# A long convolution and a gated MLP, forward and backward on one core: the filter's first transform over whole rows instead of halves, another opening, and one load moved behind another

## The chip, the cores and the metric

The kernel runs on one core of one Trainium2 chip. The metric is the device time of one execution in microseconds (us). Times in the profile are microseconds from the start of the span unless they are marked ns.

## The reference

The kernel computes the output of a block and all its gradients from a given gradient of the output. S is 2048, D is 1024, F is 3584, and everything is bfloat16 at the edges:

```python
xn = layernorm(x)                                     # [S, D]
# A: short convolution of k with 4 taps, times v, then a long convolution with a filter per channel
kv  = shift(k, shift_k) * v
y   = irfft(rfft(pad(kv)) * rfft(pad(ssm_k)))[:S] + kv * ssm_D
A   = xn * y
# B: gated MLP
gate = relu(xn @ W_gate); up = xn @ W_up
B   = (gate * up) @ W_down
out = x + A + B
# returned: out, and by vjp(grad_out) the gradients of x, k, v, shift_k, ssm_k, ssm_D, W_gate, W_up, W_down
```

## The kernel before

There are two branches in one instruction stream, and TensorE is shared by both.

The MLP branch (class LnMlp) has four phases. In `hidden`, the 3584 hidden columns are worked in 7 blocks of 512 for each half of the rows, 14 blocks in all; a block computes for each of 8 row tiles the gate product ps_g, the up product ps_u and the gradient product ps_h, each as 8 matmuls of 128x128 by 128x512 (`gemm8`, L788). ScalarE takes the relu of ps_g (L885) and copies ps_h (L958), VectorE multiplies (L891, L893, L959), and the results go to DRAM as h_d and ug_d. These products share a pool of four accumulators. The later phases are `grad_down` and `grad_in` (ps_d and ps_w, L1039 and L1052), `out_phase` (ps_o, L1197) and `grad_x` (ps_x, L1266).

The first block of `hidden` also holds the layer norm. `layer_norm` is a generator that works the 16 row tiles of x in ten chunks, `LN_CHUNKS = (1, 1, 1, 1, 2, 2, 2, 2, 2, 2)`: row sums on ScalarE (L726), centring on VectorE (L749), squares on ScalarE (L726), a root on ScalarE (L757), a few one-column operations and the scaling on VectorE (L770). In the first chunk, both sums are shared by the two engines, half a row each. `flip_xn` then transposes a row tile on TensorE (L820) and VectorE copies it to xnT (L822); the first tile is copied in two halves. Ahead of all this, `warm` runs 24 products whose results nobody reads. The loads of x wait in SP's queue in the order in which the program issues them: chunks 0 and 1, the gate weights, chunks 2 and 3, the up weights, chunk 4, four transposing loads of the down weights (wdT), two of the output's gradient (goT), chunk 5.

The convolution branch (class ABranch) works the 1024 channels in 8 groups of 128. A transform of length 4096 is done as products with tables: `fwd1` (a product with a table R over 64 rows), a transposition on VectorE (`flip`, L313), `fwd2`, products of the transforms on VectorE (`cmul`), and inverses. All its matmuls are recorded at L72, its ScalarE copies at L76, its VectorE operations at L80 and its loads at L88. The tables are made by `tables` from sines on ScalarE during the second to third block of the MLP.

The filter of a group is loaded as hn, 128 channels by 2048 times. `h_tile` brings it into the time layout: with time = 32 q + 16 u + r, the 64 rows of half u hold q, and for each r and each u the columns hv[:, u, r, :] (64 of them, 32 elements apart) are transposed into the 64 PSUM rows of that half (L302), 32 transposes in all. ScalarE copies the result to hT. `fwd1` then multiplies R[64 u : 64 u + 64] with the 64 rows of half u, 512 columns at a time; the two halves write two banks. A chunk is four such products and two copies to the tile B.

The order is set as follows. The MLP's phases yield 1730 ns for each 8 large products, and whenever a budget is used up, one step of the convolution branch is put in. A step of a group is a pair: some TensorE work and some VectorE work (`slots`, `yield f1h, tk`), worth 1760 ns. `keep_in_program_order` and `pri.pin` fix instructions in the order written, and a scheduler places the others by priority. Before the first group, `steps` issues its loads in stages:

```python
        yield 13000
        self.load_xn(nx)      # xt, the layer norm's output for this group
        self.load_taps(nx)    # skb, the four taps
        self.pin = False
        yield 9000
        self.pri.strict = True
        hT = self.h_tile(nx)
```

xt is needed by `gate_grad`, the product gt x xt on VectorE, which in the first group stands beside the first chunk of the filter; the transform of gt (f1g) reads its result.

Of the kernel before, what the change touches and what calls it, by code (L numbers as in the profile page):

```python
# [11 lines left out]
BF16 = mybir.dt.bfloat16  # L12
# [36 lines left out]
class ABranch:  # L49
# [65 lines left out]
    def tables(self):  # L115
# [4 lines left out]
        self.FW = con.tile([P, NB1, 2, NB1], BF16, name="FW")  # L120
        self.IA = con.tile([P, 16, 2, 2, NB1], BF16, name="IA")
        self.R = con.tile([P, 2, 2, NB1], BF16, name="R")
        self.RB = con.tile([P, 64], BF16, name="RB")
        self.gs_all = con.tile([P, self.NG, 4], F32, name="gs_all")
        self.gD_all = con.tile([P, self.NG], BF16, name="gD_all")
# [18 lines left out]
        b32 = pbit(32, 1.0 / 32, "b32")  # L144
        b64 = pbit(64, 1.0 / 64, "b64")
        n1 = pbit(63, 1.0, "n1p")

        def first(n, name):
            it = self.ts.tile([P, 2, 2, NB1], I32, name="it" + name, tag="ts")
# [6 lines left out]
            nc.scalar.activation(out=tr[:], in_=it[:], func=ACT.Sin, scale=TWO_PI / 256, bias=negpi[:])  # L156
            return tr

        tr = first(n1, "R")
        V.tensor_copy(out=self.R[:], in_=tr[:])  # L160

# [132 lines left out]
    def h_tile(self, st):  # L294

        hT = self.ttile("hT")
        hv = st["hn"][:].rearrange("p r c -> p (r c)").rearrange("p (q u r) -> p u r q", u=2, r=16)
        pst = self.ps.tile([P, 16, P], BF16, name="pst", tag="aps")
        for r in range(16):
            for u in range(2):  # L300
                self.pri.now()
                self.pri.pin(self.nc.tensor.transpose(pst[64 * u:64 * u + 64, r, :], hv[:, u, r, :], self.identA[:]))  # L302
        self.act(hT[:, 0:16, :], pst[:])
        return hT

    def flip(self, st, key, src):
# [4 lines left out]
        for c0 in range(0, 64, 32):  # L311
            self.pri.late()
            self.pri.pin(self.nc.vector.transpose(out=df[:, c0:c0 + 32, :], in_=sf[:, c0:c0 + 32, :]))  # L313
            yield

    def add_D(self, st):
        for rows in (slice(0, 32), slice(64, 96)):
            b0 = st["Bh"][rows, :, 0, 0, :]
            self.tt(b0, b0, st["sD"][rows].rearrange("p (cp i) -> p cp i", i=2), ALU.add)

    def fwd1(self, st, key, src):
# [136 lines left out]
    def steps(self):  # L458

        sk_t = self.shift_rows()
        self.pin = True
        nx = self.loads_1(0)
        self.loads_2(nx)
        yield 10000
        self.load(self.sk_d, sk_t[:])
        yield 13000
        self.load_xn(nx)
        self.load_taps(nx)  # L470
        self.pin = False
        yield 9000
        self.pri.strict = True
        hT = self.h_tile(nx)
        yield 2000
        for gi in range(self.NG):
            st, nx = nx, None
            for p, d in self.slots(st, hT, gi):
                self.run(p)
                self.run(d)  # L480
                yield self.SLOT
            nx, hT = st.get("nx"), st.get("hT_next")
        self.small_outputs()

    def slots(self, st, hT, gi):
# [36 lines left out]

        ksh = st["ksh"] = self.lng.tile([P, 16, P], BF16, name="ksh")
        tk = self.taps(st, ksh, kp, [(3, 0), (2, 1), (1, 2), (0, 3)])
        f1h = self.fwd1(st, "Bh", hT)
        f1g = self.fwd1(st, "Bg", gt)
        yield f1h, (lambda: self.gate_grad(st)) if gi == 0 else None
        yield None, tk
        yield f1h, tk
        yield None, tk  # L530
        yield None, self.both(lambda: self.add_D(st), tk)
        flH = self.flip(st, "fH", st["Bh"][:].rearrange("p cp u r i -> p cp (u r) i"))
        yield f1g, flH
        yield None, flH
        yield f1g, tk
# [106 lines left out]
class LnMlp:  # L642
# [66 lines left out]
    def layer_norm(self, xn_d, jpool, jtag, spool):  # L709

        nc, D, V = self.nc, self.D, self.nc.vector

        st0 = 0
        for i, n in enumerate(self.LN_CHUNKS):
            xt = self.ln_x[i]
            self.pri.now()
            sm = spool.tile([P, 12, 4], F32, name="ln_s")
            smb = spool.tile([P, 4, 4], BF16, name="ln_b")
            f = lambda i: sm[:, i, 0:n]
            b = lambda i: smb[:, i, 0:n]  # L720
            cut = D // 2 if i == 0 else D

            def row_sums(j, k, func):

                jk = jpool.tile([P, D], BF16, name="ln_j", tag=jtag)
                self.ln_act = nc.scalar.activation(out=jk[:, 0:cut], in_=xt[:, j, 0:cut], func=func,  # L726
                                                   accum_out=sm[:, k, j:j + 1])
                if cut < D:
                    if func is ACT.Square:
                        V.tensor_tensor_reduce(out=jk[:, cut:D], in0=xt[:, j, cut:D], in1=xt[:, j, cut:D], scale=1.0,  # L730
                                               scalar=0.0, op0=ALU.mult, op1=ALU.add, accum_out=sm[:, k + 6, 0:1])
                    else:
                        V.tensor_reduce(out=sm[:, k + 6, 0:1], in_=xt[:, j, cut:D], axis=AX.X, op=ALU.add)
                return self.ln_act

            def average(k, out):
                if cut < D:
                    return V.tensor_scalar(out=out, in0=f(k), scalar1=sm[:, k + 6, 0:1], scalar2=1.0 / D, op0=ALU.add,
                                           op1=ALU.mult)
                return V.tensor_scalar(out=out, in0=f(k), scalar1=1.0 / D, scalar2=None, op0=ALU.mult)  # L740

            for j in range(n):
                total = row_sums(j, 0, ACT.Copy)
                if i != 3 and i >= 1 and j == 0:
                    self.tc.keep_in_program_order(total)
            average(0, b(0))
            V.tensor_copy(out=f(1), in_=b(0))
            for j in range(n):
                V.tensor_scalar(out=xt[:, j, :], in0=xt[:, j, :], scalar1=sm[:, 1, j:j + 1], scalar2=None,  # L749
                                op0=ALU.subtract)  # L750
                row_sums(j, 2, ACT.Square)
            yield
            var = average(2, b(1))
            if i == 2:
                self.tc.keep_in_program_order(var)
            V.tensor_scalar(out=b(2), in0=b(1), scalar1=LN_EPS, scalar2=None, op0=ALU.add)
            self.ln_act = nc.scalar.activation(out=f(4), in_=b(2), func=ACT.Sqrt)  # L757
            yield
            root = V.reciprocal(out=f(6), in_=f(4))
            if i == 1:  # L760
                self.tc.keep_in_program_order(root)
            V.scalar_tensor_tensor(out=f(5), in0=b(2), scalar=0.5, in1=f(6), op0=ALU.mult, op1=ALU.mult)
            V.scalar_tensor_tensor(out=b(3), in0=f(4), scalar=0.5, in1=f(5), op0=ALU.mult, op1=ALU.add)
            self.ln_dve = V.reciprocal(out=self.rstd[:, st0:st0 + n], in_=b(3))
            self.pri.now()
            for j in range(n):
                st = st0 + j
                for c in (0, 512) if st == 0 else (0,):
                    xc = xt[:, j, c:c + (512 if st == 0 else D)]
                    V.tensor_scalar(out=xc, in0=xc, scalar1=self.rstd[:, st:st + 1], scalar2=None, op0=ALU.mult)  # L770
                nc.gpsimd.dma_start(out=xn_d[st * P:(st + 1) * P, :], in_=xt[:, j, :])
                self.xn.append(xt[:, j, :])
            st0 += n
            yield
# [39 lines left out]
    def flip_xn(self, st):  # L814
        xT = self.act_tile("xnT", st)
        h = self.DT // 2 if st == 0 else self.DT
        for k0 in range(0, self.DT, h):
            pst = self.ps.tile([P, self.DT, P], BF16, name="pst_x", tag="bps")
            for kt in range(k0, k0 + h):
                self.pri.pin(self.nc.tensor.transpose(pst[:, kt, :], self.xn[st][:, kt * P:(kt + 1) * P],  # L820
                                                      self.ident[:]), always=True)
            copied = self.nc.vector.tensor_copy(out=xT[:, k0 * P:(k0 + h) * P],  # L822
                                                in_=pst[:, k0:k0 + h, :].rearrange("p a b -> p (a b)"))
            if st < 4:
                self.tc.keep_in_program_order(copied)
        return xT
# [9 lines left out]
    def hidden(self, first, goT, load, ln, tables, Wg, Wu, Wd, g, xn_d, h_d, ug_d):  # L836
# [6 lines left out]
        for n in range(N):  # L843
# [61 lines left out]
            def first_gate_up(sp):  # L905
# [3 lines left out]
                    chunk(1)  # L909
                gate(sp)  # L910
                yield from step()
                if sp == 0:
                    next(ln)
                    next(ln)
                    next(ln)

                def mid():
                    flip(sp + 2)
                    while len(self.xn) < 4:
                        next(ln)  # L920
                    if sp == 2:
                        chunk(2)
                up(sp, mid)
                yield from step()
                gate(sp + 1)
# [53 lines left out]
                        next(ln)  # L979

            if ahead:
                self.warm(24)
                for _ in range(3):
                    next(ln)
                next(ln)
                flip(1)
                yield from first_gate_up(0)
                yield from first_gate_up(2)
                chunk()
# [419 lines left out]
```

## Time and profile before

| | |
|---|---|
| median of 4 runs | 1922.97 us (1921.47 to 1923.59) |
| the profiled execution | 1922.91 us, span 1921.1 us |
| TensorE busy | 1912.4 us, 15710 matmuls |
| VectorE, ScalarE busy | 908.6 us, 634.0 us |
| granted TensorE clock | 1.0 from 4.8 us on |
| filter transposes, L302 | 256, 278 ns each in the mean |
| filter products ps<-hT,R | 64 of 64x512, 381 ns each in the mean |
| warm-up products, L834 | 24, 460 ns each in the mean |
| hT copies on ScalarE | 8, 1.87 us each |
| VectorE waits of TensorE for xnT (L822) | 2.0 us |

A matmul's duration is the time through the array; what it takes from TensorE's stream is the distance to the start of the next one. Two half-array matmuls can be under way side by side. The chain of waits is followed back from the last instruction.

### The profile page before, as it was taken

What the parts mean: (1) busy time and instruction counts of PE and PEld (TensorE: products, weight loads), DVE (VectorE), ACT (ScalarE), POOL (GpSimd) and SP (SyncE); (2) the same over time, 40 slices, a digit from 0 to 9 for tenths busy, and PEclk for the clock granted to TensorE, in tenths of its full rate; (3) what the DMA queues carried; (4) which work ended last, traced back from release to release, by engine and by line L of the source; (5) the groups of instructions that cost most, each with busy time, mean ns of one, the idle gap of its engine ahead of it and who ended that gap; (6) DMA issues with size and microseconds to landing.
All of it is one profiled execution on the core that took longest, in us unless ns stands there. A gap on an engine that the chain in (4) does not pass through costs nothing.

```text
span 1921.1 us, 36564 instructions
## 1 busy us (share of the span) xinstructions
PE 1912.4 (100%) x15710; PEld 886.6 (46%) x15710; DVE 908.6 (47%) x1354; ACT 634.0 (33%) x865; POOL 15.0 (1%) x37
## 2 busy tenths in 40 slices
PE   9999999999999999999999999999999999999999
PEld 4444444444444444444444444444444544444444
DVE  6777777767767754534444354310122232222222
ACT  5764354364364354354344344321000000000000
POOL 1000000000000000000000000000000000000000
PEclk9999999999999999999999999999999999999999
DMA  9975778974775872645653633376999975554553
GB/s 249 285 176 143 179 184 183 229 177 131 187 184 136 250 219 78 175 128 179 162 163 92 170 99 122 100 196 219 233 261 247 225 173 121 121 121 120 121 121 72
DMA packets 628003, 323.18 MB, mean 168 GB/s; under 512 B 458360, under 2 KB 597376, under 8 KB 627840
## 3 DMA queue, kind: packets, MB, share of 16 engines
q1 hardware_dynamic: 617344, 299.99, 62.6%
q10 hardware_dynamic: 9216, 16.65, 2.9%
q0 software_dynamic: 1280, 4.20, 0.6%
q8 instruction: 123, 2.02, 0.4%
q14 instruction: 40, 0.33, 0.1%
HBM read 143.79 MB, written 95.44 MB: 125 GB/s over the span
## 4 chain that ended last, share of the span: by engine, by line
PE 96%; DVE 1%; DMA 1%; ACT 1%; issue 0%; SPq 0%; ACTq 0%; DVEq 0%
PE ps_x L1266 20%; PE ps_w L1039 20%; PE ps_o L1197 10%; PE ps_g L788 9%; PE ps_h L788 9%; PE ps_u L788 9%; PE ps_d L1039 9%; PE ps L72 6%; PE ps_d L1052 1%; PE pst L302 1%; PE ps_w L1052 1%; ACT ln_j L726 1%; DMA ln_x<-in_A_q_dram 0%; PE ps_r L1227 0%; DMA wg<-in_B_W_gate_dram 0%
## 5 line engine op out<-in xcount | busy, mean ns | idle before, releaser
L1039 PE MATMUL ps_w<-ugs,xn_nat 128*128 128x512 bf16 x1728 | 383.3, 379 | 0.0
L788 PEld LDWEIGHTS <-xnT 128*128 128x128 bf16 x1792 | 169.6, 98 | 211.6 <-issue 11.0
L1039 PEld LDWEIGHTS <-xn_nat 128*128 128x128 bf16 x1728 | 164.7, 98 | 200.2 <-issue 7.2
L788 PE MATMUL ps_g<-wg,xnT 128*128 128x512 bf16 x896 | 206.6, 379 | 2.6 <-DVE xnT L822 2.0
L1284 ACT ACTIVATE w<-xn,m 128x512 f32<-128x512 bf16 x32 | 24.3, 806 | 553.0 <-issue 317.2
L788 PE MATMUL ps_u<-wu,xnT 128*128 128x512 bf16 x896 | 206.8, 379 | 0.0
L788 PE MATMUL ps_h<-wdT,goT 128*128 128x512 bf16 x896 | 205.8, 379 | 0.3 <-ACT ru L885 0.3
L1266 PE MATMUL ps_x<-wgT,ggT 128*128 128x512 bf16 x896 | 198.6, 379 | 0.0
L1266 PE MATMUL ps_x<-wuT,guT 128*128 128x512 bf16 x896 | 198.6, 379 | 0.0
L1197 PE MATMUL ps_o<-wd,hT 128*128 128x512 bf16 (+1 forms) x896 | 187.6, 372 | 0.0
L1039 PE MATMUL ps_d<-g_nat,hs 128*128 128x512 bf16 x768 | 171.8, 379 | 0.0
L1266 PEld LDWEIGHTS <-guT 128*128 128x128 bf16 x896 | 87.7, 98 | 105.7
L1266 PEld LDWEIGHTS <-ggT 128*128 128x128 bf16 x896 | 87.7, 98 | 105.5
L1197 PEld LDWEIGHTS <-hT 128*128 128x128 bf16 x896 | 87.7, 98 | 99.9
L788 PEld LDWEIGHTS <-goT 128*128 128x128 bf16 x896 | 84.9, 98 | 103.7 <-issue 4.8
L313 DVE STREAM_TRANSPOSE flp<-C 128x1024 f32<-128x1024 f32 x48 | 90.5, 1931 | 83.4 <-ACT C L76 83.4
L891 DVE SCALAR_TENSOR_TENSOR ru<-ru,ps_u 128x512 bf16<-128x512 bf16 x112 | 76.6, 684 | 111.5 <-issue 47.5
L958 ACT CAST gh<-ps_h 128x512 bf16<-128x512 f32 x112 | 65.4, 585 | 164.9 <-PE ps_h L788 157.9
L313 DVE STREAM_TRANSPOSE flp<-B 128x1024 f32<-128x1024 f32 x48 | 90.7, 1936 | 56.9 <-ACT B L76 56.9
L1143 ACT CAST wi<-ps_w 128x512 bf16<-128x512 f32 x108 | 63.7, 590 | 162.8 <-PE ps_w L1039 153.8
L76 ACT CAST C<-ps 128x1024 bf16<-128x1024 f32 x96 | 92.5, 1015 | 68.8 <-PE ps L72 67.7
L1039 PEld LDWEIGHTS <-hs 128*128 128x128 bf16 x768 | 72.4, 98 | 89.4 <-issue 5.1
(162 smaller groups left out, 1472.6 us busy)
## 6 DMA issues: line engine op xcount, KB each, us to landing
ug_d<-ru SPq DMA_DIRECT2D x112, 256.0 KB, 4.2
ugs<-ug_d SPq DMA_DIRECT2D x112, 256.0 KB, 4.2
wg<-in_B_W_gate_dram SPq DMA_DIRECT2D x56, 256.0 KB, 3.6
wu<-in_B_W_up_dram SPq DMA_DIRECT2D x56, 256.0 KB, 5.8
h_d<-ht SPq DMA_DIRECT2D x112, 128.0 KB, 3.1
hs<-h_d SPq DMA_DIRECT2D x56, 256.0 KB, 5.2
out_dram<-wi SPq DMA_DIRECT2D x56, 256.0 KB, 2.6
gt<-in_grad_out_dram SPq DMA_DIRECT2D x32, 256.0 KB, 3.7
```

The costliest lines, as they stand in the source:

```text
L72: self.pri.pin(self.nc.tensor.matmul(out, lhsT=lhsT, rhs=rhs, start=start, stop=stop))
L76: self.pri.pin(self.nc.scalar.copy(out=out, in_=in_))
L313: self.pri.pin(self.nc.vector.transpose(out=df[:, c0:c0 + 32, :], in_=sf[:, c0:c0 + 32, :]))
L788: self.pri.pin(self.nc.tensor.matmul(ps[:], lhsT=xT[:, kt * P:(kt + 1) * P], rhs=w(kt), start=(kt == 0), stop=(kt == self.DT - 1)), always ...
L891: self.pri.pin(nc.vector.scalar_tensor_tensor(out=ru[s][:, 1, :], in0=ru[s][:, 0, :], scalar=0.0, in1=ps[:], op0=ALU.is_gt, op1=ALU.mult))
L958: self.pri.pin(nc.scalar.copy(out=gh[:], in_=ps[:]))
L1039: self.pri.pin(self.nc.tensor.matmul(ps[:], lhsT=lhsT(st), rhs=rhs(st), start=(st == 0), stop=(st == self.ST - 1)))
L1052: self.pri.pin(self.nc.tensor.matmul(ps[i][:], lhsT=lhsT(i, st), rhs=rhs(i, st), start=(st == 0), stop=(st == self.ST - 1)))
L1143: self.pri.pin(nc.scalar.copy(out=wo[0][:, d, :], in_=ps[:]))
L1197: nc.tensor.matmul(ps, lhsT=hT[:, kt, :], rhs=self.wd[:, kt, oc], start=(kt == 0), stop=(kt == self.FT - 1))
L1266: nc.tensor.matmul(ps, lhsT=T[:, kt, :], rhs=W[:, kt, oc], start=(i == 0), stop=(i == n - 1))
L1284: nc.scalar.activation(out=w[:, oc], in_=xn[:, oc], func=ACT.Identity, scale=m[:, 7:8], bias=m[:, 6:7])
```

## The change

The filter is transposed whole: with time = 16 q + r, hv[:, r, :] is 128 columns 16 elements apart, and 16 transposes fill all 128 rows. A new table RH, 128 rows by two variants, has zeros in every other row, so that a product over all 128 rows picks out the times of one parity of q. `fwd1_filter` does the filter's first transform with it: four chunks in four slots, each of two whole products and one copy. `add_D` and `flip` follow in the new layout, and the VectorE work of the first five slots is put in another order; `gate_grad` of the first group goes from the first slot to the fourth. `tables` has two more one-column masks, one more sine and two more multiplications for RH.

In `steps`, the taps are loaded where xt and the taps were loaded, and xt 9500 ns later, ahead of the first `h_tile`.

In the opening, 17 warm-up products instead of 24; the first half of the first xnT is copied by ScalarE instead of VectorE; the squares of the second chunk are shared by ScalarE and VectorE as those of the first already are; the layer norm's generator stops at two more places, and more of its instructions are kept in program order.

```diff
@@ tables
+        self.RH = con.tile([P, 2, 2, 2, NB1], BF16, name="RH")
...
+        n1h = pbit(126, 0.5, "n1h")
+        up = pbit(1, 1.0, "up")
...
+        tr = first(n1h, "H")
+        nup = lin(up, -1.0, 1.0, "nup")
+        for u, mu in ((0, nup), (1, up)):
+            V.tensor_scalar(out=self.RH[:, u], in0=tr[:], scalar1=mu[:], scalar2=None, op0=ALU.mult)
         tr = first(n1, "R")
@@ h_tile
-        hv = st["hn"][:].rearrange("p r c -> p (r c)").rearrange("p (q u r) -> p u r q", u=2, r=16)
+        hv = st["hn"][:].rearrange("p r c -> p (r c)").rearrange("p (q r) -> p r q", r=16)
         for r in range(16):
-            for u in range(2):
-                self.pri.now()
-                self.pri.pin(self.nc.tensor.transpose(pst[64 * u:64 * u + 64, r, :], hv[:, u, r, :], self.identA[:]))
+            self.pri.now()
+            self.pri.pin(self.nc.tensor.transpose(pst[:, r, :], hv[:, r, :], self.identA[:]))
@@ new
+    def fwd1_filter(self, st, hT):
+        B = st["Bh"] = self.big.tile([P, 64, NB1, 2], BF16, name="B", tag="big")
+        for r0 in range(0, NB1, 8):
+            ps = self.ps.tile([P, 1024], F32, name="ps0", tag="aps")
+            for jj in range(2):
+                r = r0 % 16 + 4 * jj
+                self.mm(ps[:, 512 * jj:512 * jj + 512], self.RH[:, r0 // 16].rearrange("p e a l -> p (e a l)"),
+                        hT[:, r:r + 4, :].rearrange("p r c -> p (r c)"))
+            self.act(B[:, :, r0:r0 + 8, :], ps[:].rearrange("p (r cp i) -> p cp r i", r=8, i=2))
+            yield
@@ steps
         yield 13000
+        self.load_taps(nx)
+        yield 9500
         self.load_xn(nx)
-        self.load_taps(nx)
         self.pin = False
-        yield 9000
         self.pri.strict = True
         hT = self.h_tile(nx)
@@ slots
-        f1h = self.fwd1(st, "Bh", hT)
+        f1h = self.fwd1_filter(st, hT)
-        yield f1h, (lambda: self.gate_grad(st)) if gi == 0 else None
+        yield f1h, tk if gi == 0 else None
+        yield f1h, tk
+        yield f1h, self.both(lambda: self.add_D(st), tk)
+        yield f1h, (lambda: self.gate_grad(st)) if gi == 0 else tk
         yield None, tk
-        yield f1h, tk
-        yield None, tk
-        yield None, self.both(lambda: self.add_D(st), tk)
@@ layer_norm
-            cut = D // 2 if i == 0 else D
+            def half(k):
+                return D // 2 if i == 0 or i == 1 and k == 2 else D
...
+            if i == 4:
+                yield
             for j in range(n):
-                V.tensor_scalar(out=xt[:, j, :], in0=xt[:, j, :], scalar1=sm[:, 1, j:j + 1], scalar2=None,
-                                op0=ALU.subtract)
+                centred = V.tensor_scalar(out=xt[:, j, :], in0=xt[:, j, :], scalar1=sm[:, 1, j:j + 1], scalar2=None,
+                                          op0=ALU.subtract)
+                if i == 4:
+                    self.tc.keep_in_program_order(centred)
+                if i == 1:
+                    yield
                 row_sums(j, 2, ACT.Square)
@@ flip_xn
-            copied = self.nc.vector.tensor_copy(out=xT[:, k0 * P:(k0 + h) * P],
-                                                in_=pst[:, k0:k0 + h, :].rearrange("p a b -> p (a b)"))
+            copy = self.nc.scalar.copy if st == 0 and k0 == 0 else self.nc.vector.tensor_copy
+            copied = copy(out=xT[:, k0 * P:(k0 + h) * P], in_=pst[:, k0:k0 + h, :].rearrange("p a b -> p (a b)"))
@@ first_gate_up
-                if sp == 0:
-                    next(ln)
-                    next(ln)
-                    next(ln)
...
-                        chunk(2)
+                        chunk(3)
@@ hidden
-                self.warm(24)
+                self.warm(17)
                 for _ in range(3):
                     next(ln)
                 next(ln)
                 flip(1)
+                for _ in range(4):
+                    next(ln)
```

More of the change, by code (lines that the diff above doesn't have):

```diff
@@ L314, in flip @@
             yield
+    def fwd1_filter(self, st, hT):
[8 more added lines that the diff above has]
+            yield
     def add_D(self, st):
         for rows in (slice(0, 32), slice(64, 96)):
-            b0 = st["Bh"][rows, :, 0, 0, :]
+            b0 = st["Bh"][rows, :, 0, :]
             self.tt(b0, b0, st["sD"][rows].rearrange("p (cp i) -> p cp i", i=2), ALU.add)
@@ L524, in slots @@
         tk = self.taps(st, ksh, kp, [(3, 0), (2, 1), (1, 2), (0, 3)])
-        f1h = self.fwd1(st, "Bh", hT)
+        f1h = self.fwd1_filter(st, hT)
         f1g = self.fwd1(st, "Bg", gt)
-        yield f1h, (lambda: self.gate_grad(st)) if gi == 0 else None
+        yield f1h, tk if gi == 0 else None
+        yield f1h, tk
+        yield f1h, self.both(lambda: self.add_D(st), tk)
+        yield f1h, (lambda: self.gate_grad(st)) if gi == 0 else tk
         yield None, tk
-        yield f1h, tk
-        yield None, tk
-        yield None, self.both(lambda: self.add_D(st), tk)
-        flH = self.flip(st, "fH", st["Bh"][:].rearrange("p cp u r i -> p cp (u r) i"))
+        flH = self.flip(st, "fH", st["Bh"][:])
         yield f1g, flH
@@ L720, in layer_norm @@
             b = lambda i: smb[:, i, 0:n]
-            cut = D // 2 if i == 0 else D
+            def half(k):
+                return D // 2 if i == 0 or i == 1 and k == 2 else D
             def row_sums(j, k, func):
+                cut = half(k)
                 jk = jpool.tile([P, D], BF16, name="ln_j", tag=jtag)
@@ L729, in row_sums @@
                     if func is ACT.Square:
-                        V.tensor_tensor_reduce(out=jk[:, cut:D], in0=xt[:, j, cut:D], in1=xt[:, j, cut:D], scale=1.0,
-                                               scalar=0.0, op0=ALU.mult, op1=ALU.add, accum_out=sm[:, k + 6, 0:1])
+                        sq = V.tensor_tensor_reduce(out=jk[:, cut:D], in0=xt[:, j, cut:D], in1=xt[:, j, cut:D],
+                                                    scale=1.0, scalar=0.0, op0=ALU.mult, op1=ALU.add,
+                                                    accum_out=sm[:, k + 6, 0:1])
+                        if i == 1:
+                            self.tc.keep_in_program_order(self.ln_act)
+                            self.tc.keep_in_program_order(sq)
                     else:
@@ L736, in average @@
             def average(k, out):
-                if cut < D:
+                if half(k) < D:
                     return V.tensor_scalar(out=out, in0=f(k), scalar1=sm[:, k + 6, 0:1], scalar2=1.0 / D, op0=ALU.add,
@@ L743, in layer_norm @@
                 total = row_sums(j, 0, ACT.Copy)
-                if i != 3 and i >= 1 and j == 0:
+                if i >= 1 and j == 0:
                     self.tc.keep_in_program_order(total)
@@ L747, in layer_norm @@
             V.tensor_copy(out=f(1), in_=b(0))
+            if i == 4:
+                yield
             for j in range(n):
-                V.tensor_scalar(out=xt[:, j, :], in0=xt[:, j, :], scalar1=sm[:, 1, j:j + 1], scalar2=None,
-                                op0=ALU.subtract)
+                centred = V.tensor_scalar(out=xt[:, j, :], in0=xt[:, j, :], scalar1=sm[:, 1, j:j + 1], scalar2=None,
+                                          op0=ALU.subtract)
+                if i == 4:
+                    self.tc.keep_in_program_order(centred)
+                if i == 1:
+                    yield
                 row_sums(j, 2, ACT.Square)
```

## The prediction

> **What bounds the kernel now.** I read the engines' shares first, then the waits, the chain, and last the timeline of TensorE around one channel group.
>
> ```profile
> PE 1912.4 (100%) x15710; PEld 886.6 (46%) x15710; DVE 908.6 (47%) x1354; ACT 634.0 (33%) x865; POOL 15.0 (1%) x37
> PE 96%; DVE 1%; DMA 1%; ACT 1%; issue 0%; SPq 0%; ACTq 0%; DVEq 0%
> PE ps_g L788 <- DVE xnT L822: 2.0, 3, 0.8
> PE ps_g L788 <- DMA wg<-in_B_W_gate_dram: 0.5, 2, 0.3
> PE ps_h L788 <- ACT ru L885: 0.3, 1, 0.3
> ```
>
> TensorE works all the time and is 96% of the chain; its listed waits are a few microseconds, all in the first 110. So a change is worth what it takes from TensorE's stream, plus those waits. Starts in the timeline price the stream (columns: start us, us, engine, line, operation):
>
> ```profile
> 230.07 3.62 PE L788 MATMUL ps_h<-wdT,goT 128*128 128x512 bf16 x16
> 233.61 1.99 PE L302 MATMUL pst<-ident,hn 128*64 128x128 bf16 x32
> 235.54 1.90 PE L788 MATMUL ps_g<-wg,xnT 128*128 128x512 bf16 x8
> 237.28 0.63 PE L72 MATMUL ps<-RB,flp 128*128 128x64 bf16 x16
> 237.74 1.89 PE L788 MATMUL ps_g<-wg,xnT 128*128 128x512 bf16 x8
> 239.47 1.89 PE L788 MATMUL ps_u<-wu,xnT 128*128 128x512 bf16 x8
> ...
> 243.39 1.89 PE L788 MATMUL ps_h<-wdT,goT 128*128 128x512 bf16 x8
> 245.21 0.61 PE L72 MATMUL ps<-hT,R 64*128 64x512 bf16 x4
> 245.75 1.90 PE L788 MATMUL ps_h<-wdT,goT 128*128 128x512 bf16 x8
> ```
>
> A whole-array product of 512 columns costs (239.47 - 237.74)/8 = 0.216 us. The 32 half transposes of the filter cost 235.54 - 233.61 = 1.93 us, and they began at 233.61 where sixteen products of 0.216 from 230.07 end at 233.53: 0.09 us is lost in going from the whole array to half of it. Together 2.02. Four half-array products of the filter cost 0.54 plus the same 0.09, so 0.63: two run side by side, for four alone would be 0.86. The 128x64 products from 237.28 stay in the whole array, load 128 new columns each, and cost 0.46/16 = 0.029 each, with no loss at entry.
>
> **The change, part by part.**
>
> *Transposes.* Eight groups now pay 8 x 2.02 = 16.2 us. Afterwards there are 16 whole transposes per group, no half-array mode and no 0.09. Their price is the unknown, since no row has a whole-array load of columns that lie apart in memory. The lower bound is the transposes of the opening:
>
> ```profile
> 12.28 0.62 PE L820 MATMUL pst_x<-ident,ln_x 128*128 128x128 bf16 x8
> 12.68 0.59 PEld L788 LDWEIGHTS <-xnT 128*128 128x128 bf16 x4
> 12.73 1.03 PE L788 MATMUL ps_u<-wu,xnT 128*128 128x512 bf16 x4
> L302 PEld LDWEIGHTS <-hn x256: 185/204/209, 94.3 to 1119.3; 128*64 128x64 bf16 x128
> L72 PEld LDWEIGHTS <-IA x3072: 101/101/105, 158.0 to 1249.4; 32*64 32x64 bf16 x192
> ```
>
> (12.73 - 12.28)/8 = 0.056 us each, with adjacent columns. The last two rows are loads of 64 columns: 101 ns where they are adjacent, 204 where they are strided by 64 bytes (the filter). A pair of half transposes takes about 0.111 us (1.93 x 2/32, less the tail), twice a transpose's 0.056, so the strided load sets their pace. If 128 strided columns cost what such a pair costs, 0.111; if one stream has to carry what two carried, 0.223. I take 0.056: the whole-array rows load 128 columns in at most 0.029, about a quarter of what a pair needs for as many strided columns, and even at half that speed a load stays under 0.056. That gives 8 x 16 x 0.056 = 7.2, a gain of 9.0; the ends are 14.3 (gain 1.9) and 28.5 (loss 12.3).
>
> The Trainium skill ("TensorE: Matmul & The Clock Gate", weight-path perf modes) says that loads of 128 columns run as four parallel chunks, packed or strided, which would make a transpose 0.056. Against the change speaks "SBUF — State Buffer" (specifications): reads that change their 16-byte line at each element fall below full bandwidth; the 204 ns row agrees, and if that held for the four chunks together the price would be the 0.111.
>
> *Filter products.* Before, 16 chunks of 0.63 = 10.1 us, and 0.2 more in the first group, where the first product waits for the copy of hT (97.98 to 98.28, of which 0.09 is the mode). After: RH has zeros for the other half, so all 64 products are whole: 64 x 0.216 = 13.8. Loss 3.7. The first wait grows: the transposes end sooner and the next 1.73 us of products too, while the copy of 1.87 us on ScalarE starts only at their end; I put the wait at 0.4, a loss of 0.2. Results are copied one tile per slot, 1 us on ScalarE in a slot of 1.76, so they hide; if they did not, the two accumulators would stall TensorE by up to 0.5 us a slot.
>
> *The convolution input xt.* Now SP issues it between the first and the second piece of the third block's gate weights, and the rest of these go out 5 us later:
>
> ```profile
> 93.48 0.58 SPq L781 DMA_DIRECT2D wg<-in_B_W_gate_dram  x1
> 95.95 1.36 SPq L88 DMA_DIRECT2D xt<-xn_d  x2
> 97.36 1.32 SPq L88 DMA_DIRECT2D skb<-sk_d  x1
> 98.79 1.41 SPq L781 DMA_DIRECT2D wg<-in_B_W_gate_dram  x3
> 103.87 0.59 PE L788 MATMUL ps_g<-wg,xnT 128*128 128x512 bf16 x2 [0.34 <-DMA wg<-in_B_W_gate_dram]
> ```
>
> TensorE loses 0.52, 0.34 and 0.24 us in this block against 0.216 a product: 1.1. Afterwards the taps' load skb goes ahead of two stores of ug_d, all four gate pieces follow each other, then one store of h_d, then xt, then the up weights. The gate pieces leave by 96, land by 101 at the latest (5 us, as here) and are wanted at 103: gain 1.1. What queues behind xt is wu, issued at 100.8 now and no later then, with the store of h_d ready by 96. The product gt x xt moves from the first to the fourth slot on VectorE; its reader comes two slots (3.5 us) after it, and one pass takes 1.23. Cost nothing; 1 us if VectorE is late.
>
> *ScalarE before the first group.* The extra table RH (two passes over 128 elements, one sine of 0.4) hides, but it changes the order on ScalarE. Now two relus stand together at 84.97, and the second h block loses 85.60 - 85.11 = 0.49 waiting for one of four accumulators. In the changed order the second of these relus stands behind a table sine (0.65) and two passes of the layer norm (2.1). By the rows' durations that relu ends at 88.4, where its accumulator is wanted at 87.1: 1.3, and 0.2 at 81.7, against 0.49 now. Loss 1.1; bounds 0 and 1.4.
>
> *Opening.* Seven products of the warm-up go (these have already reached full clock: the last one starts at 8.08, and the layer norm is ready at 8.03). Half of the first copy moves to ScalarE. Gate products start at about 9.1 instead of 9.44, and the squares of the second tile, split over two engines, save 0.1. But look what the chain does next:
>
> ```profile
> 21.10 6.19 DMA ln_x<-in_A_q_dram
> 27.37 2.20 ACT ln_j L726 x4
> ...
> 32.14 3.63 PE ps_g L788 x16
> ```
>
> The sixth load of x stands on SP behind four transposing loads (7.98 to 18.11) and two more, none of which waits for TensorE. It lands at 27.3, and the copies that release 32.14 follow it. All that is won before is waited for there. I book 0, bounds -0.5 and +0.3.
>
> **Sum.** -9.0 + 3.7 + 0.2 - 1.1 + 1.1 + 0 = -5.1 us. The profiled execution took 1922.91 us (span 1921.1), the median of the runs is 1922.97: **1917.8 us**. Nothing else of the change touches the later stages.
>
> **Rivals.**
> 1. *The strided load sets the pace* (0.111): the transposes gain 1.9 only, and -1.9 + 3.7 + 0.2 = +2.0 gives 1924.9, slower. It decides from (16.2 - 3.9)/128 = 0.096 us a transpose on. For it: the 204 ns row; against it: the quick whole-array loads. Its extreme, one stream, 0.223: +16.2, so 1939.
> 2. *The opening's gain passes, and ScalarE's order does no harm*: -0.5 and -1.1 more, about 1916.2. Against it: the chain through the load of x.
> 3. *In between* (0.07 to 0.1): -3.3 to +0.5, about 1921.4.
> 4. *The load of xt is not what made the gate weights late* (the table of windows has a DMA share of 1.04 from 98 to 110): 1.1 back, 1918.9.
>
> **How the numbers follow.** My sum with rival 4: 0.50 (its own range 1916.3 to 1919.6). Rival 2: 0.10. In between: 0.13. Load at 0.111: 0.18. One stream: 0.09. Two tenths of a per cent are 3.8 us, about what a measurement of this kernel can tell: faster than 1919.1 are rival 2 and nearly nine tenths of the sum's 0.50, 0.54. Slower than 1926.8 are the single stream and a quarter of the 0.111 case with its unknown waits: 0.14. The rest, 0.32, lies within. The range 1915.8 to 1925.8 leaves out the single stream, and a tenth of the rest.
>
> **What would show it.** Right: 16 transposes taking 0.9 us and no 0.09 ahead of them; two whole products per chunk at 0.43; no wait for wg near 103; a wait for ScalarE near 87; ps_g still starting at 32.1. Wrong: transposes at 1.8 or 3.6 a group, loads of hn above 200 ns still, or ps_g before 31.8.

## The result, and the profile after

The changed kernel takes 1920.07 us (median of 31 runs, 1918.34 to 1924.48), the kernel before 1922.94 us on the same chip (51 runs, 1921.47 to 1924.42). The medians differ by 2.9 us. The ratio, 0.9988 with an interval of 0.9983 to 0.9993 (0.12% faster), is nearer to that of the means (1920.55 and 1922.94, 2.4 us apart), since the changed kernel's runs reach further up than down. The profiled execution took 1919.38 us with a span of 1917.3, so the two profiles differ by 3.8 us of span.

The page and the waits of TensorE in the changed kernel, against the lines shown of before:

```profile
PE 1908.1 (100%) x15575; PEld 886.0 (46%) x15575; DVE 910.7 (48%) x1365; ACT 635.4 (33%) x868; POOL 15.8 (1%) x38
PE 97%; DMA 1%; DVE 1%; ACT 0%; SPq 0%; issue 0%; DVEq 0%; ACTq 0%
```

```profile
PE ps_g L818 <- DVE xnT L853: 1.8, 2, 1.5
...
PE ps_u L818 <- DMA wu<-in_B_W_up_dram: 0.9, 2, 0.5
```

TensorE still sets the time. There are 135 matmuls fewer: 128 transposes and 7 warm-up products. The wait for the gate weights wg has gone, and two waits for the up weights wu have come, near 62 and near 106; the wait of ps_g for xnT holds 1.5 us in one piece. The timeline of TensorE around the first group (start, duration through the array, what) shows the new pieces:

```profile
92.50 1.89 PE L818 MATMUL ps_u<-wu,xnT 128*128 128x512 bf16 x8
94.23 1.17 PE L308 MATMUL pst<-ident,hn 128*128 128x128 bf16 x16
95.24 1.89 PE L818 MATMUL ps_u<-wu,xnT 128*128 128x512 bf16 x8
97.35 0.59 PE L72 MATMUL ps<-hT,RH 128*128 128x512 bf16 x2 [0.23 <-ACT hT L76]
97.78 1.89 PE L818 MATMUL ps_h<-wdT,goT 128*128 128x512 bf16 x8
...
106.62 4.50 PE L818 MATMUL ps_u<-wu,xnT 128*128 128x512 bf16 x16 [0.48 <-DMA wu<-in_B_W_up_dram]
```

The transposes follow the products without a gap and take 95.24 - 94.23 = 1.01 us, 0.063 each. A chunk of the filter takes 97.78 - 97.35 = 0.43. The sixteen up products near 106 take 4.50 where others take 3.6: besides the wait at their start there are gaps between them, 1.53 us in all (0.64, 0.30, 0.31 and 0.28, from the distances of the starts). Waits of TensorE are given in this way from here on; where a trace lacks the record of one of the sixteen products, the 0.22 us of that product is taken off. Each trace is one execution. SP's queue shows where the up weights stood:

```profile
93.77 2.29 SPq L811 DMA_DIRECT2D wg<-in_B_W_gate_dram  x4
...
96.88 1.88 SPq L88 DMA_DIRECT2D xt<-xn_d  x2
98.86 5.22 SPq L811 DMA_DIRECT2D wu<-in_B_W_up_dram  x4
```

SP needs 5.22 us to issue the four pieces of wu, 2.7 of it for the first: behind xt, whose two loads have 1024 packets of 256 bytes each, the issuing instruction itself is held up. In all 13 profiles of this case, the first piece of wu takes 1.6 to 3.4 us to issue in the seven in which it stands behind xt, and 0.38 to 0.39 in the six others. Last, the chain of waits in the opening:

```profile
21.84 5.39 DMA ln_x<-in_A_q_dram
27.32 2.20 ACT ln_j L746 x4
...
32.09 3.63 PE ps_g L818 x16
```

The sixth load of x lands at 27.3 as before, and ps_g starts at 32.09 where it started at 32.14.

### The profile page after: what moved, and what is told of

Read it like the earlier page. It is cut to its first block, busy times and chain, and to the rows that moved or that the text cites. A ratio compares the mean times of both kernels' runs of the same rounds, so it can differ in the third digit from the quotient of the medians.

```text
span 1917.3 us, 36312 instructions
## 1 busy us (share of the span) xinstructions
PE 1908.1 (100%) x15575; PEld 886.0 (46%) x15575; DVE 910.7 (48%) x1365; ACT 635.4 (33%) x868; POOL 15.8 (1%) x38
## 4 chain that ended last, share of the span: by engine, by line
PE 97%; DMA 1%; DVE 1%; ACT 0%; SPq 0%; issue 0%; DVEq 0%; ACTq 0%
PE ps_x L1294 20%; PE ps_w L1067 20%; PE ps_o L1225 10%; PE ps_h L818 10%; PE ps_u L818 10%; PE ps_g L818 10%; PE ps_d L1067 9%; PE ps L72 7%; PE ps_d L1080 1%; PE ps_w L1080 1%; DMA wu<-in_B_W_up_dram 1%; DMA ln_x<-in_A_q_dram 0%; PE pst L308 0%; PE ps_r L1255 0%; ACT ln_j L746 0%
## 5 line engine op out<-in xcount | busy, mean ns | idle before, releaser
L1294 PEld LDWEIGHTS <-ggT 128*128 128x128 bf16 x896 | 87.7, 98 | 105.5
```

The source lines that it names most:

```text
L1294: nc.tensor.matmul(ps, lhsT=T[:, kt, :], rhs=W[:, kt, oc], start=(i == 0), stop=(i == n - 1))
```

## The experiments

The theory after the result: the transposes and products account for -8.1 + 3.7, the opening brings nothing because of the load of x, and the block of weights near 103 to 109 pays back part of the gain, since xt and the traffic ahead of it now delay the up weights. Rivals: the halves' price came from half-array mode and not from the spacing of the columns; the opening did matter; the order on SP has no part in it. The kernel before took 1922.94 to 1923.35 in all sets; each ratio below is to its runs on the same chip.

| run | what differs from the changed kernel | median (range), us | ratio [interval] |
|---|---|---|---|
| changed kernel | | 1920.07 (1918.3 to 1924.5) | 0.9988 [0.9983, 0.9993] |
| after_again | nothing | 1920.72 (1918.1 to 1924.2) | 0.9989 [0.9980, 0.9998] |
| no_opening | opening of before | 1919.80 (1918.8 to 1921.8) | 0.9981 [0.9972, 0.9990] |
| open_only | kernel before, with the opening alone changed | 1923.34 (1922.0 to 1925.2) | 1.0004 [0.9995, 1.0012] |
| xt_late | xt behind wu | 1920.55 (1918.3 to 1924.2) | 0.9987 [0.9978, 0.9996] |
| x6_early | sixth load of x earlier | 1920.95 (1918.6 to 1923.1) | 0.9989 [0.9980, 0.9998] |
| vt_late | vt behind wu | 1919.16 (1918.3 to 1921.9) | 0.9981 [0.9972, 0.9989] |
| vt_x6 | vt_late and x6_early | 1919.06 (1917.3 to 1920.6) | 0.9980 [0.9971, 0.9989] |
| vt_xt | vt_late and xt_late | 1919.07 (1917.9 to 1921.2) | 0.9980 [0.9972, 0.9989] |
| vt_xt_x6 | all three | 1919.35 (1917.5 to 1921.7) | 0.9980 [0.9971, 0.9989] |
| vt_xt_noopen | vt_xt, opening of before | 1918.95 (1917.7 to 1920.2) | 0.9978 [0.9970, 0.9987] |

### What a transpose costs: stride_look

```diff
-        hv = flat.rearrange("p (q r) -> p r q", r=16)       # spacing 16 in every group
+        step = (16, 1, 2, 4, 8, 16, 16, 1)[st["gi"]]        # groups 6 and 7: pairs of 64 columns
+        hv = flat.rearrange("p (b q s) -> p b s q", q=P, s=step)
```

> The changed kernel with another spacing of the transposed columns in each of the eight channel groups, to price a transpose by itself. Groups 0 and 5: 128 columns with a spacing of 16 elements as changed; groups 1 to 4: 128 columns with a spacing of 1, 2, 4 and 8; group 6: pairs of 64 columns with a spacing of 16, as before the change; group 7: pairs of 64 adjacent columns. The columns of groups 1 to 4, 6 and 7 then stand in another order, so that these groups compute another filter; counts and sizes of everything else are the same. Measured from the trace alone: time from the first transpose to the first product behind, over 16. Theory 1, the spacing costs a little in the load of 128 columns and sets the pace of the halves: 63 ns at spacing 16, 56 at 1, a step somewhere between; halves 111 to 121 a pair with spacing 16 and 56 to 63 a pair when adjacent. Theory 2, half-array mode itself sets the pace of the halves: 111 to 121 a pair for group 7 as well. Theory 3, the 7 ns between 56 and 63 are not the spacing but what else a group does (its copies, the reads of hn): 63 at all six spacings of whole transposes.

From the timeline of TensorE: groups 1 (spacing 1), 4 (spacing 8) and 7 (pairs of 64 adjacent columns), each with the products behind:

```profile
235.71 1.06 PE L311 MATMUL pst<-ident,hn 128*128 128x128 bf16 x16
236.61 1.68 PE L829 MATMUL ps_g<-wg,xnT 128*128 128x512 bf16 x7
...
673.32 1.15 PE L311 MATMUL pst<-ident,hn 128*128 128x128 bf16 x16
674.30 1.89 PE L829 MATMUL ps_h<-wdT,goT 128*128 128x512 bf16 x8
...
1117.43 1.08 PE L318 MATMUL pst<-ident,hn 128*64 128x128 bf16 x32
1118.44 1.90 PE L1078 MATMUL ps_w<-ugs,xn_nat 128*128 128x512 bf16 x7
```

The loads of the columns themselves (min/median/max in ns), in groups 1, 4, 5, 6 and 7:

```profile
L311 PEld LDWEIGHTS <-hn x16: 97/98/98, 235.5 to 236.5; 128*128 128x128 bf16 x16
L311 PEld LDWEIGHTS <-hn x16: 143/146/151, 673.1 to 674.2; 128*128 128x128 bf16 x16
L311 PEld LDWEIGHTS <-hn x16: 145/148/160, 821.9 to 823.0; 128*128 128x128 bf16 x16
L318 PEld LDWEIGHTS <-hn x32: 194/218/223, 970.9 to 972.7; 128*64 128x64 bf16 x32
L318 PEld LDWEIGHTS <-hn x32: 106/110/111, 1117.4 to 1118.2; 128*64 128x64 bf16 x32
```

| | spacing, elements | per transpose or pair |
|---|---|---|
| whole | 1, 2, 4 | 0.056 us (0.893 to 0.894 for 16) |
| whole | 8 | 0.061 (0.983) |
| whole | 16 | 0.063 (1.005 in groups 0 and 5) |
| pair of halves | 1 | 0.063 (1.016) |
| pair of halves | 16 | 0.131 (2.091) |
| pair of halves, before | 32 | 0.120 (1.93) |

Theory 1 holds, but for the pairs with spacing 16, which cost 0.131 where 0.111 to 0.121 was expected. For whole transposes the spacing costs 5 to 7 ns, from 8 elements (16 bytes) on; for halves it doubles the price. The loads show that whole loads aren't spared: they go from 98 ns to 148 (113 at spacing 4), half as long again, but of these 50 ns only 7 reach the pace of the transposes. The 64-column loads go from 110 to 218. Half-array mode by itself sets no such pace: adjacent halves cost about what a whole one does, and only the 0.09 at the entry on top. Theories 2 and 3 fall.

### The opening: no_opening, open_only, x6_early

`no_opening` has `warm(24)`, `flip_xn` and `layer_norm` of before in the changed kernel; `open_only` has the changed ones in the kernel before; `x6_early` moves one line:

```diff
-    goT = [b.load_T(g, i, "goT", 8 + i) for i in range(2)]
     load(5)
+    goT = [b.load_T(g, i, "goT", 8 + i) for i in range(2)]
```

> The changed kernel with the opening of before (24 warm-up products, whole first copy on VectorE, the layer norm's old order); the filter's transposes and products and the place of xt as changed. Theory 1, the opening's gain ends at the load of x that lands at 27.3: the median is that of the changed kernel, 1920.1 within 0.4, gate products start at 32.1, and the wait for up weights near 106 is there too (0.5 to 1.5 us). Theory 2, something of the opening reaches the end: 1920.6 or more. Theory 3, the wider scatter of the changed kernel comes from its shorter warm-up: here the runs lie within 3 us again and the median is lower, about 1919.3.

> The kernel before with the opening alone changed (17 warm-up products, half of the first copy on ScalarE, the layer norm's new order); filter and xt as before. Theory 1, its gain is swallowed at the load of x that lands at 27.3 (gate products at 32.1 in both): the median of the kernel before within 0.4, with a wait ahead of these products that is 0.5 to 0.8 longer than the 0.93 of before. Theory 2, the new order of the layer norm helps the first group too (the 0.49 us that a relu cost near 85): 0.4 to 0.8 faster. Theory 3, the shorter warm-up widens the scatter: runs more than 4 us apart.

> The changed kernel with the sixth load of x issued on SP ahead of the first two transposing loads of goT instead of behind them (one line); the order on all other engines is unchanged. Theory 1, this load alone holds the opening's gain back: it is issued at about 18.1 instead of 21.8 and lands by 24; the copy of xnT that released the gate products at 32.09 then starts when its transposes end (29.7), the wait ahead of these products shrinks from 1.67 us to 0.5 or less, and the median falls by 0.9 to 1.4 to about 1918.9. Theory 2, the copy is held by the order on VectorE and ScalarE whatever the load does: wait of 1.2 us or more, gain under 0.4.

In `no_opening` the gate products start at 10.45 instead of 9.13, as 14 of the 24 warm-up products ran at half rate, and yet ps_g starts at 31.52 without a wait, ahead of the 32.09 of the changed kernel (theory 1 expected 32.1). In this execution the sixth load of x landed at 26.0. In the nine other profiles with that load in its old place, it lands between 27.0 (`vt_late`) and 28.1 (`vt_xt_noopen`), and ps_g starts about 4.85 us later in each: the load decides, and it moves between executions. The median is 0.3 below that of the changed kernel, which is within theory 1, and nothing for theory 2. But the kernel before is 0.4 slower on this chip, and by the ratios, 0.9981 against 0.9988, the changed kernel is faster without its opening; against the 22 runs of `xt_late` and `x6_early`, on the same chip and with the opening, the median is 0.9 lower (by resampling 0.1 to 2.3). The runs lie within 3 us. So theory 3 can't be put aside for the changed kernel. `open_only` gains nothing, as theory 1 has it, and its runs lie within 3.2 us, against theory 3. The relu's 0.49 near 85 is gone there too, but it doesn't show in the median. Its profile has something new. First the timeline of TensorE, then a table of windows (length, TensorE busy, granted clock, DMA share, GB/s):

```profile
32.84 5.31 PE L801 MATMUL ps_g<-wg,xnT 128*128 128x512 bf16 x15 [2.28 <-DVE xnT L836]
```

```profile
33.00:34.00 1.00, 1.00 (x5) 1.00 1.27 243
...
35.00:36.00 1.00, 1.00 (x4) 0.50 1.21 259
```

The wait for xnT is 2.4 us instead of 0.93, where theory 1 expected 0.5 to 0.8 more: 0.8 of it because the products ahead were done earlier, 0.7 because the load landed at 28.0 instead of 27.3. After this wait the granted clock fell to 0.5 for about 3.4 us: these products took 5.15 us (32.84 to 37.99) instead of 3.46.

`x6_early`: the load is issued at 18.32, and

```profile
30.97 2.33 PE L818 MATMUL ps_g<-wg,xnT 128*128 128x512 bf16 x9 [0.32 <-DVE xnT L853]
```

The wait falls from 1.67 to 0.49 and ps_g starts 1.1 us earlier, as theory 1 expected; the median does not follow (theory 1 expected -0.9 to -1.4; the ratio is that of the changed kernel). Compared with the changed kernel's profile instruction by instruction, this one is 1.7 us ahead at 81, 2.25 at 110, but 1.2 at 396 and 0.7 at 488, and 0.6 at the end: near 393 TensorE waits 0.99 us for wu and near 486 0.57 for wg, which the changed kernel's profile doesn't have. So in this execution most of the lead was paid back at later blocks of weights. It wasn't at each: near 62 it doesn't wait for wu, and near 106 for 0.9 us instead of 1.53. And it is the fastest of its 11 runs, so that it doesn't show why their median gains nothing.

### The up weights: xt_late, after_again, vt_late

`xt_late` issues xt one step into the first group, behind wu; `vt_late` does so with vt, six steps in.

```diff
-        self.load_xn(nx)                # xt_late: in steps()
-        vt = ...; self.load_time(vt, self.v, cg)   # vt_late: in loads_2(), first group
...
             for n, (p, d) in enumerate(self.slots(st, hT, gi)):
+                if gi == 0 and n == 1: self.load_xn(st)    # xt_late
+                if gi == 0 and n == 6: self.load_v(st)     # vt_late
```

> The changed kernel with xt issued on SP behind the four pieces of the up weights instead of ahead of them; nothing else is moved on any engine. Theory 1, xt ahead of wu is what made TensorE wait 1.5 us for wu (0.64 + 0.30 + 0.31 + 0.28) between 105.8 and 108.5: these waits fall below 0.4 in all; gt x xt on VectorE starts when xt lands, about 110 instead of 106.2, and products of gt that start at 111.05 now wait 0 to 1.0: gain 0.5 to 1.5, median 1918.6 to 1919.6. Theory 2, the DMA engines are full from 85 to 108 whatever the order, and wu is late by its own size: waits for wu of 1 us or more remain, and a wait for gt of about 1 us comes on top: 1920.1 to 1921.

> The changed kernel itself, timed again on the chip of the three others of this set, to have its place and its scatter there. Every theory: 3 us below the kernel before on this chip (2.3 to 3.5), single runs 5 us or more apart; in the trace, weights waited for near 106, and an earlier arrival at that place paid back there.

> The changed kernel with the two loads of vt of the first group (1024 packets of 256 bytes each, 512 KB) issued behind the up weights, at about 111 instead of 82; they are wanted at 128. Nothing moves on the compute engines. Theory 1, from 85 to 108 the DMA engines are full, and the up weights come late because of what is queued before them: vt takes about 2.5 us of these engines, so the waits for wu between 104 and 109 (1.1 to 1.7 us in four profiles) fall below 0.3, and the median by 0.8 to 1.5. Theory 2, wu comes late because xt stands right ahead of it on SP: waits of 1.1 to 1.7 remain, median unchanged within 0.4.

`xt_late`: the order on SP is not enough. The four pieces are issued from 97.41 to 100.10, without being held up (the first takes 0.39), and still TensorE waits 0.51 + 0.80 us for them, and then 1.0 for gt x xt. Theory 2, so far.

`after_again` shows how far the same program can move. From SP's queue and TensorE's timeline of its profiled execution (1922.45 us):

```profile
87.12 1.31 SPq L88 DMA_DIRECT2D vt<-in_A_v_dram  x2
...
97.83 2.34 SPq L811 DMA_DIRECT2D wg<-in_B_W_gate_dram  x4
```

```profile
106.18 2.32 PE L818 MATMUL ps_g<-wg,xnT 128*128 128x512 bf16 x10 [1.14 <-DMA wg<-in_B_W_gate_dram]
...
109.96 1.11 PE L818 MATMUL ps_u<-wu,xnT 128*128 128x512 bf16 x3 [1.03 <-DMA wu<-in_B_W_up_dram]
```

Here vt is issued at 87.1 instead of 82.0, eleven stores queue behind it, and wg comes at 97.8 instead of 93.8. TensorE waits 2.07 us for wg and 2.07 for wu, 4.1 in all against 1.53 in the first profile. With 0.4 more for up weights near 62 and 0.3 in the opening this accounts for the 3.3 by which the two profiles' last products differ.

`vt_late` takes these 512 KB out of the queue. SP then has nothing to issue from 88.4 to 91.8, wg is issued at 93.5, and the waits fall to 0.19 + 0.29. The median is 1.56 lower than that of `after_again` on the same chip (by resampling the 11 runs of each: 0.0 to 3.3). Theory 1, though 0.5 us of waits remain where less than 0.3 was expected: here the first pieces of wu stood behind xt again.

### Both, and the rest: vt_x6, vt_xt, vt_xt_x6, vt_xt_noopen

These have the edits above put together.

> The changed kernel with both: the first group's vt behind the up weights, and the sixth load of x ahead of the transposing loads of goT. Theory 1, what the earlier x gains (1.2 at 32) was paid back at the weights near 106 in the run without vt moved (0.5 of it later, near 395 and 488); with the queue relieved more of it stays: 1.0 to 2.5 below the changed kernel's median on this chip. Theory 2, each earlier arrival is paid back at the next block's weights whatever the queue: within 0.5 of the changed kernel.

> The changed kernel with the first group's vt behind the up weights (issued near 111) and xt behind the up weights too; nothing moves on the compute engines. Theory 1, two things made wu late: the queue ahead (vt) and SP held up behind the 2048 small packets of xt (the first wu piece took 2.7 us to issue). With both gone wu is issued from 96 to 99 and lands before it is wanted at 105: no wait for wu above 0.2, xt lands by 107 and holds nothing (products of gt start at 109). About 0.7 below the run with vt alone moved: ratio to the kernel before 0.9976 to 0.9979, and runs within 3 us of each other. Theory 2, wu's own 1 MB behind the 1 MB of wg is what takes the time: waits of 0.5 or more for wu remain, plus up to 1 us for xt: ratio 0.998 or above.

> The same with the sixth load of x ahead of the transposing loads of goT as well. Theory 1, what is won at 32 (0.7 to 1.3) now stays to the end, less up to 0.9 us where goT lands late (near 26 to 28): 0 to 1.0 below the run without it, ratio 0.9972 to 0.9978. Theory 2, it is paid back at the weights near 57 to 62, near 106 or near 395 and 488: same ratio within 0.0002.

> The first of these three with the opening of before (24 warm-up products and the old layer norm): filter as changed, vt and xt behind the up weights. Theory 1, the opening is worth nothing even with the queue relieved, as the load of x at 27 decides where the gate products start: ratio within 0.0002 of the first. Theory 2, it is worth 0.5 us or more, one way or the other.

SP's queue and TensorE's timeline of `vt_xt`:

```profile
97.18 2.35 SPq L818 DMA_DIRECT2D wu<-in_B_W_up_dram  x4
```

```profile
106.86 3.62 PE L825 MATMUL ps_u<-wu,xnT 128*128 128x512 bf16 x16
```

Sixteen up products in 3.62 us without a wait, in this run and in the two with it, where `xt_late` waits 1.3 us and `vt_x6`, with vt alone moved, 1.4: that both causes were there, the queue ahead and SP held up behind xt, fits this. It isn't shown cleanly, since these three want wu at 106.4 to 106.9 and `xt_late` at 105.5: part of the missing wait is a later reader. But the time does not fall by as much: all five versions lie between 0.9978 and 0.9981. `vt_xt` then waits 0.5 for gt x xt and 0.6 for a transposed tile near 127; `vt_x6` waits 0.9 for goT near 26 to 28, which its sixth load of x went past, and 1.2 for weights near 57 to 62; `vt_xt_x6` waits 2.1 for those. So theory 2 is right of `vt_xt_x6` (same ratio) and theory 1 of `vt_xt_noopen` (within 0.0002). For `vt_xt` the wait for wu was gone as theory 1 had it, and the ratio of theory 2 was measured. `vt_x6` is 1.7 below `after_again`, as its theory 1 had it, but `vt_late` without the earlier load of x is 1.6 below.

The five versions' 55 runs have a median 1.2 us below the 42 of the changed kernel (by resampling 0.5 to 1.8). The best is the filter of the change without its opening, and with vt and xt behind the up weights: 0.9978 [0.9970, 0.9987], runs within 2.5 us. That one of the five beats another is not shown. Nor is it shown that they beat `no_opening` (0.9981), which leaves vt and xt in their places: the 1.2 us are against the kernel with its changed opening.

## Why the prediction was right or wrong

The predicted 1917.8 was 2.3 below the median, inside the range (1915.8 to 1925.8), and "faster by over 0.2%", which had 0.54, did not come: 0.12% lies in the case given 0.32. By its terms, in the two profiles:

| term | predicted | measured |
|---|---|---|
| transposes | -9.0 | -8.1 |
| filter products | +3.7 | +3.7 |
| first wait for hT | +0.2 | +0.2 |
| wg near 103 | -1.1 | -1.1 |
| wu behind xt | 0 | +1.5 |
| ScalarE's order | +1.1 | -0.5 |
| opening | 0 | 0 |
| up weights near 62 | not named | +0.5 |
| sum | -5.1 | -3.8 |

*Transposes.* Right in kind and short in size. "I take 0.056" should have been 0.063: 8 x 16 x 0.007 = 0.9 us. The load at 0.111 and the single stream did not come. `stride_look` shows why the pair was no guide: the spacing doubles the 64-column loads (110 to 218 ns) and their price, while it lengthens the 128-column loads by half (98 to 148) and the transposes by an eighth. The reason given, that whole loads have a reserve, holds in the main, but from a spacing of 8 elements on the longer load shows in the price.

*Filter products, first wait.* As worked out: 0.431 for a chunk, 0.39 for the wait.

*Gate weights.* The wait was gone in this profile, and the rival that xt had no part in it is not supported by it. But 2.1 us were waited for wg in `after_again`, where its issue began at 97.8 instead of 93.8, so that this gain holds in some executions and not in others.

*What queues behind xt.* This step failed: "What queues behind xt is wu, issued at 100.8 now and no later then" and "Cost nothing; 1 us if VectorE is late". The start of the issue was indeed earlier, 98.86, but its end was later (104.1 instead of 103.5), and the products that want wu came 1.5 us earlier (105.98 against 107.47) because of the time that had been saved ahead of them. I had compared the issue with its own old time and not with the new time of its reader, and I had counted an issue as instantaneous. VectorE, on the other hand, was in time.

*ScalarE's order.* Wrong in sign. I had placed the table sines later than they came; the layer norm's passes began at 80.77 and both relus were in time (82.86 and 86.08), so that the old stall of 0.49 went and no new one came. The bounds of this term, 0 and 1.4, had left out a gain without a reason.

*Opening.* Right that it gains nothing: without it nothing is lost, alone it brings nothing, and the start of ps_g follows the landing of the load of x. That the changed kernel is even faster without it (0.9981 against 0.9988) was not foreseen, and the reason is open. With the load of x moved, 1.1 us do get through to ps_g, and 0.6 of it is left at the end of that profile.

*The sum.* That it came within 1.3 us of the profile is partly luck: the transposes (0.9), wu behind xt (1.5) and the up weights near 62 (0.5) cost 2.9 more than forecast, and ScalarE's order cost 1.6 less.

Of the remaining 0.9 between the profile's -3.8 and the median's -2.9, 0.7 is that the profiled execution lay below the median of a kernel that scatters more: 6.1 us over 31 runs against 3.0 over 51 before. The two profiles of it differ by their waits for loads alone (0.3 for x, the rest for weights), and with vt moved the range shrinks to between 2.5 and 4.2; that these waits make the scatter is likely from this, and not shown run by run. Why `no_opening` scatters less than the changed kernel while its waits near 106 are 1.3, nearly the same, stays open.

## What to carry to other kernels

A microsecond saved on the bounding engine brings forward the time at which the next weights are wanted, so look at each load between the saving and the end: issue time plus landing time against the new time of its reader, and not against its own old time. A load with many small packets takes time of the DMA engines and, as here, microseconds of the queue that issues it; put such loads where the engines have room (here behind 110, with a share of 0.3 up to 116), and not into the stage that is already full. Saving ahead of a wait that something else ends only makes the wait longer.

## What the runs showed of the hardware

- Column spacing in a transpose: for 128 columns the load takes 98 ns at a spacing of 1 or 2 elements, 113 at 4, 146 at 8 and 148 at 16, and the transposes follow each other at 0.056 us up to 4 elements, 0.061 at 8 and 0.063 at 16; pairs of 64 columns cost 0.063 adjacent and 0.12 to 0.13 apart. The Trainium skill ("SBUF — State Buffer", specifications) puts the limit at two reads in each 16-byte line. The place of the step agrees (4 elements leave the pace as it was, 8 don't); how much it costs depends on whether 64 or 128 columns are loaded.
- The half rate at the start ended between 4.2 and 7.4 us in 13 profiles, after 6 to 14 slow products; so 24 warm-up products ended between 8.5 and 9.7, and 17 between 6.7 and 8.2. The Trainium skill ("TensorE: Matmul & The Clock Gate", Part 1) says that this varies from run to run with the phase of a free-running window, and the profiles agree.
- A wait of 2.4 us in mid-run was followed by half the clock for 3.4 us, and cost 1.7 us; waits of up to 2.1 us (`vt_xt`) were not. This was seen once.
- An issue on SP can take microseconds: a store right behind the two loads of xt took 4.5 us to issue in `xt_late`, 5.4 in `vt_xt`, 4.7 in `vt_xt_x6` and 2.8 in `vt_xt_noopen`, where others take 0.4.
